# An attention and gated-MLP kernel: the scaling of p on GpSimd by two row scalars, an addition moved to GpSimd, more engines for float64 pieces, and new order tables

## The chip, the cores and the metric

The kernel runs on one core of one Trainium2 chip. The metric is the device time of one execution in microseconds. Three runs of the kernel before took 406.78, 407.47 and 408.01 us; the median is 407.47 us.

## The reference

```
# q, k, v: (4 batches, 8 heads, 768, 64) float32; n_global = 8, n_local = 96
scores = q @ k.T / 8 - slope[h] * dist     # dist: distance, n_local for global keys
scores = where(key < n_global or 0 <= row - key < n_local, scores, -1e9)
a = exp(scores - max); a = a / (sum(a) + 1e-9)
x = (a @ v) laid out as (4, 768, 512)
h = gelu_tanh(x @ w_in)                    # w_in: (512, 1024) float64
u, v = halves of h
v_n = (v - mean) / sqrt(var + 1e-6) * g_ln # layernorm over 512
v_s = w_sg @ v_n + b_sg                    # w_sg: (768, 768), over the sequence
out = x + (u * v_s) @ w_out                # w_out: (512, 512) float64
```

w_in and w_out arrive as float64 and are turned into float32 on the chip.

## The kernel before, in words

Attention is done in 48 units: a unit is one batch, one pair of heads and two blocks of 128 rows. For a unit TensorE makes the scores in 64x64 quarters (line 1115); VectorE adds the bias, finds the row's extreme and writes p (line 1147); ScalarE takes exp and the row sums (line 1152); a small operation adds 1e-9 to the sums (lines 1159 to 1163), VectorE takes the reciprocal (line 1165); and then p's four pieces, each 128 rows by 128 or 168 columns, are multiplied by it, one row scalar for each row. Each of the four may go to GpSimd (line 1174), ScalarE (line 1172) or VectorE (line 1177). In the first 16 units (`TURNS = 16`) p is then transposed by TensorE (line 1236) and copied out of PSUM (lines 1241, 1242); later units are transposed in blocks by VectorE and DMAs. The products with v are line 1264.

The gated MLP of a batch follows its attention and is mixed with the attention of the next batch. Each float32 operand is held as a high and a low part, so a product is three matmuls (lines 576 to 578). `norm` makes v's tile: gelu, statistics on VectorE (lines 633, 634), an addition of 4e-6 (line 635), the power -0.5 and a product on GpSimd (lines 640, 641), the normalization, and the split into z. The last batch's product with w_out is done by seven products of blocks instead of eight (`seven`, lines 824 to 826); its results are added up by VectorE from PSUM (line 836, and for x's low half line 717, VectorE or GpSimd) and stored (line 846).

`load_split` brings a piece of a weight matrix. A float64 piece of 256 or 512 columns is loaded as words; ScalarE multiplies the upper words by 2^-112 (line 927); the 16 bits beside are copied (line 932, GpSimd or VectorE); VectorE shifts and joins (lines 936, 938). Then any piece is cast to its high part (lines 940 to 942), and the rest becomes its low part (line 943). w_in comes in four pieces of 512 and eight of 256 columns, w_out in eight of 256.

The order of all work is planned in Python before the program is written. An operation (`op`) lists the engines that may do it, each with a busy time and a latency that the planner is told. `Plan.order` walks through time and lets each engine take the waiting operation that is due first, on the engine that would end it first. Two tables steer it, with one character for each of the 2612 operations: SHIFTS moves an operation in the order, and WAYS fixes an engine by a letter (P for GpSimd, D, A) or leaves it open with "-". Ways named DVE_SB, DVE_TS, POOL and POOL_TS count as using the port that VectorE and GpSimd share: the planner keeps such work of the two engines apart, and in the program a GpSimd operation of that kind waits for the VectorE operation before it ("beside VectorE"). POOL_FREE does not hold the port and gets no such wait. While TensorE would wait in the first 75 us, `keep_on` puts in products with a column of zeros (line 512). ALIGNED sets the address of TensorE's code at one place; HINTED places two branch hints near the end.

Of the kernel before, what the change touches and what calls it, by code (L numbers as in the profile page):

```python
# [10 lines left out]
F32 = mybir.dt.float32  # L11
# [5 lines left out]
ALU = mybir.AluOpType  # L17
PSUM = bass.MemoryType.PSUM

P = 128  # L20
# [31 lines left out]
HINTED = ("DVE", 100, mybir.EngineType.DVE), ("PE", 16, mybir.EngineType.PE)  # L52
ALIGNED = 86, 232
# [12 lines left out]
    "LJ0b0XJM0eA0ccV3WXFtrkNLJPNBzF-FhqNNAe2a0eJXbD0C201PKrBnf-6J1QojnW2wfVKTvELgvf1avq45VV30K18Hwfz2OkO5b0dc00ZN"  # L66
    "MZWw9n4-oUxuckTXWIeThmq5IKlV-50O4VtS-j0dmo94U2mZ000JHtHns-xfD4QQ67J64jZ0F57R00w4vodyM8eh09s0Do35X4F16SE1ntVO"
    "E-u4KT46E5V0ZUb8woA8RJU6RMrB0Vup-Z6rQ80doSPV5ur----8--yTKZ-t---n--v2BBt7oj00000Y4R5m5hNUzCuRldRjts7x-g-yT-nv"
    "9iQ1WZku8ml8bnSe0LswyuV0z1--l7y--C2mg--M5q--pWcx9i9V04iBLAzpTIE0Pb16sjtanFsWclFX9GLMHSZEJJKgGdI5k2-Rtjk84hMy"
    "Nr5-sPpQ-75vtIGtFFTtUrxdGbrY-KYrfadRvcS8rqlWGiWDDU3bJRJL5qz0bvcvvxxaDrt3PFRDAtRuupblR-vJQJ7uFRrmXd00M3eWtF2f"  # L70
    "1p1L23GVp18LmG4Ys1OccgKJ-h1-RBC16u8f3Y1Y-bDM-67ER5PZSI0NhhBDSRC9w3Q6aagO9l-Scgpw-Lj8YCw1crW1wl-eKRq7-sQeRx5m"
    "lFGV0ayIU5NIsUa4XNtouxHb-X0Kd3510YAcf6NB69jpSJW-smSAw0g0awTSdOVzdAZ49eaQYVaFFF68EeJYH-ubr0Bd0XWca0g-I9-F0-13"
    "16P04LPKt0w0FG160wsfiUuT-k-k7eGgZW-lcDTj8u-6qi9M3QY1F0Qlm0LoO0005038BzvdGsvT450-t--Zr--f---y-y-V-qjdUsONBnS3"
    "G9dWv-c9fU-mW0l6TlptOJX3NR-d-Oa-9NkWAOeKA6DBBgL4AABDAkFG4WpyGwaocSO-esWFHQ0O8Dccnk04rlQzmHWhYQUz-S8U0BHU07yK"
    "3krSIbGr--B7Okc-zdywZf0Z004kkA9WykrfGAfcWeWPL5Fm0OMVntcDhr069fJXhwosU2o0nxT9M9Yzrz-P-UzVfYdcvJL1CCG-1NSrOTvr"
    "d-UJshGqmYK6vJ-0Lv00f1PmjjImM1OoNNe7Bh8CJnCd0okgfs3h80Osh100nilYA9Cc7A-6bYWRMgF0SiUFBePOyz-w-qrnJFr--O-M7Xhj"
    "sUIhtF5FiG7F0T0wFt-vyWQa2Nq6skk30907DS2v09Og595u0FMa06ym8MkGj5GVKtBpvaQaXEsyTTUO80-tucRXtf9P430-7H1F-Aa90k0R"
# [8 lines left out]
    "dkknY8ndEP1Yt0MkLtb0ahHVpsxN8sy8Zbg65AG-r7Ie-I-s6PS2p-0cRUOaW5S2-cbguayZH828d1Fj---yXt--bU9X5jmAF--c0DviNbNe"
    "Uu-VGwkZO-L-EII-UeGSLd0S6pps-MdaRMbJJ-UKf02902bv-Z67vOBH0bHuzuvrZYmKpmKbnWyQs0xCxEWh5lFcHLE0X2V8K5A29308qGEu"
    "i087I-Q7j-Z7PdxtSt1alYoBiUa4ZElKzmIS0IKTW0pk9UOSO0vfKNiR7T-IcmTGxuC0jbukopGLeofaeWEWZMbsWsH00000-nG0Db0008lC"
    "kyQarbqijX5u9PFqWJuSlbBMlVl4I1BkJttKO2BQHMhJ3oNxu8YCgKIBG005JNHEcxt9GabMMLnHq20xlaakpx3T8TwFK3yDbO-lxf54UytL"
    "-G4V7OYo-eTvzcFMsY-Z"  # L90
# [27 lines left out]
    "-----D----D---------"
# [434 lines left out]
class Moe:  # L553
# [72 lines left out]
    def norm(self, t, ps):  # L626
# [85 lines left out]
    def sbuf(self, out, a, b, how, cols, reads):  # L712

        nc, op = self.nc, self.plan.op

        def one(eng):
            eng.tensor_tensor(out.ap, a(), b(), how)

        op([on_dve_sb(cols) + (partial(one, nc.vector),), on_pool(cols) + (partial(one, nc.gpsimd),)], reads, [out])
# [82 lines left out]
    def seven(self, x, dst, late):  # L802
# [13 lines left out]
        def product(n, i, left, right, on=None, after=None):  # L816
# [913 lines left out]
```

## Time and profile before

| | |
|---|---|
| median of three runs | 407.47 us |
| the profiled execution's own time | 406.97 us |
| its span, first to last instruction | 405.2 us |
| mean granted TensorE clock | 0.994 |
| TensorE busy | 396.0 us, 98% |
| VectorE busy | 345.5 us, 85% |
| ScalarE busy | 224.9 us, 56% |
| GpSimd busy | 198.9 us, 49% |

PE is TensorE's matmuls, PEld its weight loads, DVE VectorE, ACT ScalarE, POOL GpSimd and SP SyncE, which issues the DMAs. Matmuls are pipelined, and their ends are modelled, so a busy PE is not necessarily a PE at its peak. L1174 is line 1174 of the kernel.

### The profile page before, as it was taken

Reading aid. Unit: us, or ns where it says so; the run is one execution under the profiler, and the core shown is the slowest. Engines: PE = TensorE matmul, PEld = TensorE weight load, DVE = VectorE, ACT = ScalarE, POOL = GpSimd, SP = SyncE. Lnnn points to the kernel's source line nnn. Section 1 sums busy time; section 2 is a strip of 40 time slices with the busy share of each in tenths; the row PEclk is TensorE's granted clock in tenths of the full one; section 3 lists DMA queues with packets and bytes.
Section 4 is the critical chain, followed back from the end, with each engine's and each line's share of the span. In section 5 each row is a group of like instructions: output and inputs, shape, how many; then the busy total and the mean of one; then the engine's idle time right before and its main releaser. Section 6 shows DMA issues by size and latency. Waiting matters only on the chain.

```text
span 405.2 us, 12620 instructions
## 1 busy us (share of the span) xinstructions
PE 396.0 (98%) x4629; PEld 362.8 (90%) x4629; DVE 345.5 (85%) x1149; ACT 224.9 (56%) x736; POOL 198.9 (49%) x335
## 2 busy tenths in 40 slices
PE   7989999999999999999999999999999999999995
PEld 4868778999999889999999988999999888999995
DVE  7898999999998999987876989977667677878995
ACT  5899999865565657654534666725344233421300
POOL 3455788875455684332222454416221363594532
PEclk9899999999999999999999999999999999999999
DMA  7875765445878886837487665745277442000003
GB/s 231 294 177 163 232 198 169 140 130 174 258 232 264 243 274 203 247 97 232 140 255 225 199 185 153 216 111 165 64 215 245 119 141 51 20 1 2 0 21 142
DMA packets 50115, 67.14 MB, mean 166 GB/s; under 512 B 5888, under 2 KB 34048, under 8 KB 50048
## 3 DMA queue, kind: packets, MB, share of 16 engines
q1 hardware_dynamic: 50048, 66.28, 53.7%
q8 instruction: 38, 0.62, 0.7%
q14 instruction: 29, 0.24, 0.2%
HBM read 47.91 MB, written 18.35 MB: 164 GB/s over the span
## 4 chain that ended last, share of the span: by engine, by line
PE 88%; ACT 5%; DVE 4%; issue 1%; DMA 1%; POOL 0%; DVEq 0%; ACTq 0%; POOLq 0%
PE mm_ps L576 24%; PE mm_ps L578 23%; PE mm_ps L577 23%; PE av L1264 8%; PE s_ps L1115 6%; ACT p L1152 2%; PE tps L1236 2%; DVE p L1147 1%; PE mm_ps L826 1%; PE mm_ps L825 1%; PE mm_ps L824 1%; ACT p L1172 1%; DMA ni<-in_n_gl_dram 1%; ACT pt L1241 1%; ACT stage L927 1%
## 5 line engine op out<-in xcount | busy, mean ns | idle before, releaser
L1152 ACT ACTIVATE p<-p,pst 128x168 f32<-128x168 f32 (+1 forms) x192 | 80.9, 424 | 36.4 <-DVE pst L1147 35.3
L576 PE MATMUL mm_ps<-wsg,z 128*128 128x384 f32 x192 | 65.4, 340 | 0.0
L578 PE MATMUL mm_ps<-wsg,z 128*128 128x384 f32 x192 | 64.3, 335 | 0.0
L577 PE MATMUL mm_ps<-wsg,z 128*128 128x384 f32 x192 | 64.3, 335 | 0.0
L1147 DVE CUSTOM_DVE_ANT_0 p<-s_ps,bias 128x168 f32<-128x168 f32 (+1 forms) x192 | 54.3, 317 | 4.2 <-PE s_ps L1115 1.7
L1174 POOL TENSOR_SCALAR p<-p,pst 128x168 f32<-128x168 f32 (+1 forms) x87 | 40.1, 471 | 26.3 <-DVE pst L1165 20.7
L1264 PE MATMUL av<-pt,v 64*64 64x128 f32 (+1 forms) x1408 | 49.0, 253 | 0.6 <-ACT pt L1241 0.5
L1264 PEld LDWEIGHTS av<-pt,v 64*64 64x64 f32 x1408 | 37.6, 135 | 8.6 <-issue 3.7
L576 PE MATMUL mm_ps<-x,win 128*128 128x384 f32 x128 | 43.5, 340 | 0.0
L578 PE MATMUL mm_ps<-x,win 128*128 128x384 f32 x128 | 42.9, 335 | 0.0
L577 PE MATMUL mm_ps<-x,win 128*128 128x384 f32 x128 | 42.9, 335 | 0.0
L1115 PE MATMUL s_ps<-qk 64*64 64x64 f32 (+2 forms) x1408 | 38.8, 241 | 0.1
L576 PE MATMUL mm_ps<-win,x 128*128 128x512 f32 x96 | 38.8, 404 | 0.0
L578 PE MATMUL mm_ps<-win,x 128*128 128x512 f32 x96 | 37.8, 394 | 0.0
L577 PE MATMUL mm_ps<-win,x 128*128 128x512 f32 x96 | 37.7, 393 | 0.0
L576 PEld LDWEIGHTS mm_ps<-wsg,z 128*128 128x128 f32 x192 | 36.0, 188 | 1.8 <-issue 1.2
L1115 PEld LDWEIGHTS s_ps<-qk 64*64 64x64 f32 x1408 | 34.0, 135 | 3.4 <-issue 1.9
L1152 ACT ACTIVATION_READ_ACCUMULATOR p<-p,pst 128x1 f32 x192 | 36.6, 191 | 0.0
L577 PEld LDWEIGHTS mm_ps<-wsg,z 128*128 128x128 f32 x192 | 36.0, 188 | 0.3
L578 PEld LDWEIGHTS mm_ps<-wsg,z 128*128 128x128 f32 x192 | 36.0, 188 | 0.0
L593 ACT ACTIVATE u<-mm_ps 128x384 f32<-128x384 f32 x32 | 15.6, 488 | 32.7 <-PE mm_ps L578 32.4
L576 PE MATMUL mm_ps<-gt,wout 128*128 128x384 f32 x96 | 32.7, 340 | 0.0
(196 smaller groups left out, 987.7 us busy)
## 6 DMA issues: line engine op xcount, KB each, us to landing
qk<-in_qk_in_dram SPq DMA_DIRECT2D x32, 328.0 KB, 4.2
pt<-far SPq DMA_DIRECT2D x24, 384.0 KB, 4.7
v<-in_v_in_dram SPq DMA_DIRECT2D x32, 256.0 KB, 3.5
far<-tt SPq DMA_DIRECT2D x52, 96.0 KB, 2.6
qk<-in_qk_in_dram SPq DMA_DIRECT2D x16, 276.0 KB, 4.0
out_dram<-o SPq DMA_DIRECT2D x23, 192.0 KB, 3.2
far<-stage SPq DMA_DIRECT2D x44, 96.0 KB, 2.5
v<-in_v_in_dram SPq DMA_DIRECT2D x16, 192.0 KB, 3.4
```

Of the source, the lines that this page charges most:

```text
L576: mm(ps.ap, ah, bh, start=(i == 0), stop=False)
L577: mm(ps.ap, ah, bl, start=False, stop=False)
L578: mm(ps.ap, al, bh, start=False, stop=(i == n - 1))
L593: op([on_act(n) + (lambda: nc.scalar.activation(out.ap, h.ap, AF.Square, scale=math.sqrt(GELU_C * GELU_A)),)], [h], [out])
L824: mm(ah, bh, start=not on and r == 0, stop=False)
L825: mm(ah, bl, start=False, stop=False)
L1115: nc.tensor.matmul(s_ps[h][e * HQ:(e + 1) * HQ, i * W + c0:i * W + c0 + n], qk[rows, qc:qc + HQ], qk[rows, QW + k0:QW + k0 + n], start=Tru ...
L1147: nc.vector.tensor_tensor_reduce(out=p[:, g, cols], in0=s_ps[h][:, i * W:i * W + nk], in1=bias[:, 2 * j + h, w0:w0 + nk], op0=ALU.add, op1 ...
L1152: op([on_act(nk, 0.225) + (lambda p=p, g=g, cols=cols, i=i: nc.scalar.activation(p[:, g, cols], p[:, g, cols], AF.Exp, bias=st[:, 0, i, g: ...
L1174: op([on_pool_ts(nk) + (partial(scaled, lambda o, a, c: nc.gpsimd.tensor_scalar(o, a, c, 1.0, ALU.mult, ALU.mult)),), on_act(nk, 0.13) + ( ...
L1236: nc.tensor.transpose(tps[:, a * P:(a + 1) * P], pc[:, c:c + P], ident)
L1264: nc.tensor.matmul(to, v[rows, vc:vc + D], of, stop=True, skip_group_check=True, **kw)
```

## The change

- In the first 16 units the scaling of p on GpSimd multiplies by two row scalars, the reciprocal and a column of ones (`w.one`), instead of by the reciprocal and the constant 1.0; the planner is told POOL_FREE and a longer time for it. Later units keep the old form.
- The addition of 4e-6 in the layernorm moves from VectorE to GpSimd.
- The multiplication of a float64 piece by 2^-112 may also go to VectorE or GpSimd, and the copy of its 16 bits also to ScalarE.
- For the fourth product of the last batch the halves of x are added in advance into the buffer of the result (`whole_x`, not before the TensorE operation that stands just ahead of the product in the program), so that one addition from PSUM is left.
- SHIFTS, WAYS, ALIGNED and HINTED have new values. 2556 of the 2612 characters of SHIFTS differ.

```diff
-HINTED = ("DVE", 100, mybir.EngineType.DVE), ("PE", 16, mybir.EngineType.PE)
-ALIGNED = 86, 232
+HINTED = ("DVE", 101, mybir.EngineType.DVE), ("PE", 16, mybir.EngineType.PE)
+ALIGNED = 97, 139
...
-            nc.vector.tensor_scalar(rs[:, 0:1], mv[:, 1:2], 4e-6, None, ALU.add)
-
-        op([on_dve(FF, 0.40) + (stats,)], [g], [st, mv, rs])
+
+        op([on_dve(FF, 0.24) + (stats,)], [g], [st, mv])
 
         def power():
+            nc.gpsimd.tensor_scalar(rs[:, 0:1], mv[:, 1:2], 4e-6, None, ALU.add)
...
-        op([("POOL_FREE", 0.92, 1.0, power)], [mv], [rs])
+        op([("POOL_FREE", 1.14, 1.22, power)], [mv], [rs])
...
+                if r == 0 and ahead:
+                    ahead(i, [next(o for o in reversed(self.plan.ops) if o.quarters is not None)])
...
+        def whole_x(i, after):
+            kept[4, i] = self.temp("o", CH)
+            self.sbuf(kept[4, i], x_of(2 + i, 0, 0), x_of(2 + i, 0, 1), ALU.add, CH, [x[2 + i][0]], after)
+
         def fourth(i, ps):
-            o = self.temp("o", CH)
-            plus_x(o, 2 + i, 0, ps)
+            o = kept[4, i]
+            plus(o, lambda: o.ap, ps, [])
             store(o, 2 + i, 0)
...
+        def scaled(eng):
+            eng.tensor_scalar(f.ap, words()[:, :, 1].bitcast(F32), 2.0 ** -112, None, ALU.mult)
+
         op([on_act(n, 0.07) + (lambda: nc.scalar.mul(
-            f.ap, words()[:, :, 1].bitcast(F32), 2.0 ** -112),)], [raw], [f])
+            f.ap, words()[:, :, 1].bitcast(F32), 2.0 ** -112),),
+            ("DVE_TS", 0.07 + n / 1850, 0.15 + n / 1350) + (lambda: scaled(nc.vector),),
+            ("POOL_TS", 0.19 + n / 438, 0.22 + n / 438) + (lambda: scaled(nc.gpsimd),)], [raw], [f])
...
-            ("DVE_TS", 0.065 + n / 1400, 0.25 + n / 960) + (partial(beside, nc.vector.tensor_copy),)], [f], [raw])
+            ("DVE_TS", 0.065 + n / 1400, 0.25 + n / 960) + (partial(beside, nc.vector.tensor_copy),),
+            on_act(n) + (partial(beside, nc.scalar.copy),)], [f], [raw])
...
                 op([on_pool_ts(nk) + (partial(scaled, lambda o, a, c: nc.gpsimd.tensor_scalar(
-                        o, a, c, 1.0, ALU.mult, ALU.mult)),),
+                        o, a, c, 1.0, ALU.mult, ALU.mult)),) if n >= TURNS else
+                    ("POOL_FREE", 0.12 + nk / 255, 0.15 + nk / 255) + (
+                        partial(scaled, lambda o, a, c: nc.gpsimd.tensor_scalar(
+                            o, a, c, w.one, ALU.mult, ALU.mult)),),
```

The letters of WAYS that the prediction speaks of, in the order of the operations:

```
scaling of p, first 14 units (56):   before A 9, D 12, P 16, open 19    after A 21, D 14, P 6, open 15
scale of float64 pieces 0 to 7:      before ScalarE only                after DD-D--P-
copy of 16 bits, pieces 0 to 7:      before -D-DPPD-                    after -AAAA-A-
high part, w_in pieces 0 to 7:       before -AAA-AAA                    after ---A--P-
```

## Rows read from the trace of the kernel before

**Rows 1.** The page: busy us, share of the span and instructions of each engine.

```profile
PE 396.0 (98%) x4629; PEld 362.8 (90%) x4629; DVE 345.5 (85%) x1149; ACT 224.9 (56%) x736; POOL 198.9 (49%) x335
```

**Rows 2.** Busy time by stretch: start:end, length, busy time and instructions per engine.

```profile
10.00:62.00 52.00, 49.93 (x965) 40.06 (x964) 48.31 (x216) 49.63 (x180) 32.78 (x60) 0.97 0.67 209
85.00:110.00 25.00, 25.00 (x247) 24.16 (x247) 24.22 (x78) 13.61 (x45) 15.09 (x21) 1.00 0.57 173
62.00:400.60 338.60, 338.57 (x3575) 318.48 (x3573) 288.96 (x893) 169.70 (x540) 162.72 (x250) 1.00 0.52 158
```

**Rows 3.** The same view, line 512 (zero column) alone: PE and PEld.

```profile
10.00:62.00 52.00, 6.93 (x86) 5.77 (x86) 0.97 0.67 209
```

**Rows 4.** Waits: who waited for whom; us in total, times, longest.

```profile
PEld tps L1236 <- POOL p L1174: 3.0, 3, 1.8
...
PE tps L1236 <- POOL p L1174: 2.3, 2, 1.4
```

**Rows 5.** Timeline of the end: start, duration, engine, line, operation.

```profile
400.11 0.55 DVE L836 TENSOR_TENSOR kept<-kept,mm_ps 128x384 f32<-128x384 f32 x1
...
400.23 0.34 PE L826 MATMUL mm_ps<-late,wout 128*128 128x384 f32 x1
...
400.68 0.55 DVE L836 TENSOR_TENSOR o<-x,mm_ps 128x384 f32<-128x384 f32 x1
...
401.26 0.56 DVE L717 TENSOR_TENSOR o<-o,x 128x384 f32<-128x384 f32 x1
401.85 0.33 SPq L846 DMA_DIRECT2D out_dram<-o  x1
```

**Rows 6.** Scalings of p to 62 us by line: count, ns min/median/max, first and last start.

```profile
L1174 POOL TENSOR_SCALAR p<-p,pst x18: 375/410/1055, 9.3 to 57.9; 128x168 f32<-128x168 f32 x16, 128x128 f32<-128x128 f32 x2
L1172 ACT ACTIVATE p<-p,pst x20: 396/421/467, 9.2 to 58.8; 128x168 f32<-128x168 f32 x17, 128x128 f32<-128x128 f32 x3
L1177 DVE TENSOR_SCALAR p<-p,pst x18: 274/302/584, 9.5 to 55.4; 128x168 f32<-128x168 f32 x11, 128x128 f32<-128x128 f32 x7
```

**Rows 7.** Groups on POOL, 10:62: busy us, mean ns, idle before, releasers.

```profile
L1174 POOL TENSOR_SCALAR p<-p,pst 128x168 f32<-128x168 f32 x15 | 6.4, 433 | 1.9 <-DVE win L943 0.8 <-DVE pst L1165 0.7
...
L648 POOL TENSOR_SCALAR vg<-vg,mv,rs 128x512 f32<-128x512 f32 x1 | 2.1, 2091 | 0.0
...
L641 POOL TENSOR_SCALAR rs<-mv,rs 128x1 f32<-128x1 f32 x3 | 0.9, 295 | 0.3
```

**Rows 8.** Timeline, POOL and DVE side by side at 11 and at 49 us.

```profile
11.13 1.34 POOL L932 COPY stage<-stage 128x512 int16<-128x512 int16 x1 [0.29 <-ACT stage L927]
...
11.96 0.58 DVE L1177 TENSOR_SCALAR p<-p,pst 128x128 f32<-128x128 f32 x1
...
49.25 2.09 POOL L648 TENSOR_SCALAR vg<-vg,mv,rs 128x512 f32<-128x512 f32 x1
...
49.69 0.63 DVE L1177 TENSOR_SCALAR p<-p,pst 128x168 f32<-128x168 f32 x2
```

**Rows 9.** Groups on ACT, 10:62, columns as in rows 7.

```profile
L1172 ACT ACTIVATE p<-p,pst 128x168 f32<-128x168 f32 x16 | 6.5, 427 | 0.0
...
L927 ACT ACTIVATE stage<-stage 128x512 f32<-128x512 f32 x4 | 2.7, 670 | 0.0
...
L940 ACT CAST win<-stage 128x512 fp32r<-128x512 f32 x3 | 1.9, 624 | 0.0
L927 ACT ACTIVATE stage<-stage 128x256 f32<-128x256 f32 x4 | 1.6, 426 | 0.0
...
L940 ACT CAST win<-stage 128x256 fp32r<-128x256 f32 x3 | 1.2, 403 | 0.0
```

**Rows 10.** Busy time by stretch, line 932 alone: DVE, then POOL.

```profile
10.00:62.00 52.00, 2.25 (x4) 4.39 (x4) 0.97 0.67 209
```

**Rows 11.** Groups on DVE, 10:62, columns as in rows 7.

```profile
L936 DVE TENSOR_SCALAR stage<-stage 128x512 int32<-128x512 int32 x4 | 1.6, 424 | 0.2
...
L635 DVE TENSOR_SCALAR rs<-mv 128x1 f32<-128x1 f32 x3 | 0.5, 153 | 0.1
```

More of the change, by code (lines that the diff above doesn't have):

```diff
@@ L86 @@
[L86 to L90, printed above, removed]
+    "4lTyOXWL7-sM13fBP0a1V65-bt94s0KaTK95Hg0Mk--o8BiEAbV-i0G0Lgm1V6pge9Gi0pmeeRiGsrovVZbenVpC82090qhLN-rioOAutn3f"
@@ new lines @@
+    "w0JZRBp9r3b7kwjOr3U0dLn0ZBCUl-N0lcPO7UZq-zm0rXQdH2AN20gSY2qpniIsmDfXZEI8APPr-GVeTOurpoYUJvYaRc0b40BS0WB8bnf6"
+    "nwn4L109Rt0L-3Jw0XLDY4o9Lk0cJ2DSE05E340ZLHhfZFCclASWtwxdnI0nEnUQxGXnqGjQ4a8-nzNF-iqYVXzpW2p-iqYpwUSS7ww0I00H"
+    "H0FZ00DGXtGe8TC0JxSVDsydmdm-ratAieEMZA1VpW12eR-9fBGpRt2E035K2FhXXkwqTT3PKdoiG-OZ8O0HZrmHifsdqUMufauD-DBaz5L0"
+    "dg5DblMeL0XBpTK4y1a3Kma-HEebS-zv-Tu-wY4-BzCD-tFq-IIGbZyw-fgZSchlbWB8KIsZN95a0920b0hbe2kZ0bc02Ue0n0000n0LpBj1"
+    "2hTQ6FWpcr6Amh7CuiDtmYe7-8tvW4iBk-SxtkvVQMFxquUe7-flw-xOxnte6oMSZXNjmJPV6BMA7c0w-00TeYKZwclkG-t5d5FySgDJ4A4L"
@@ new lines @@
+    "XAU4Iz00abUBBJ-vZxKtAt8Bdpb0DUeQyzml-WiBG6u6zNpy-qg2Y-5NqXzfTYYZNVUm0XmQLOlgiUOJPWrDoYqRNwVE4ZWg-gTos8y-m-tX"
+    "TnlJCI0q0D48-befLOhk9SX4X407U-KWZiSW-sLPI0m0CtNEVcWHYOC0Ysal5WFhhEeIWG4Tug-DyycIVyCwz-acdF8aQvwsTDpIuT5fNibE"
+    "-toVKm1buerfSLIGZUCHuFuvaoIxjoG0SrsOxRKGyV--poYvuS7bpOFdOV0VGkSQfd70gJIR0GmBlopqn--uz-h7lmqnuoi6aYS-MjW9upDo"
+    "aWLtaksDGbC-m0AunHFv-OX6wwLdv-fz7rSTdq1-nPNEUyic1nKcXhUam6pKs6Oa-CpqOIiazzCnPgSlz41y99-AvFlb1K7a2sjWLRGdea-6"
+    "0-SfWkaSu2lCETJj6bGw7TLjN8b0W36eDDyPyyyYI6im9s5chwliVZST50vDsb9kI8dBKP5vdMMSXUvHbWGkaDvWQC7wE0jURUah-luelSXR"
@@ new lines @@
+    "tWZBVvBZgWKLKtT0ZOG93PH5U0AGGEtNWj57emqM9SeGRS0Mub02900PJKDgR0NWcPzz-Z80oQBYWFY0v-Geqz4JOVkGEr0V6ZPL--LtC-a-"
+    "cT-v8VlIn-Fqu7gJ0QUIpqidiKbXPU0wdHZ2AGKIZ-el-kAxkqNe0al3-0fLYL-RVZfaMYlHs1syVCJU05e-iAIQNMGtv1L20U3OK4Rc6xY0"
+    "2SlLDEa0doBsWfkPnD0a5NR5-0gI-71020W0E0f4ogrgTcdcamh-0N60iOjv60rVKanq202ZRRRSPFTDaW400bMeSNLSJMXUoKDgAE0dPfaC"
+    "lNeQSEmWJtAe0Ti0iidtBQufAFx-MuiBose081x0clXRY0JFeFeGAT010oRLRQ0-S3PpIbV8-HZI8-04H5O0M23K0nN0Klp03Xa0c0Doa0HK"
+    "d8cvSw8fi-9ajbhXDaQRKjJ27XhDML409RLUclQVZ0B00oB0mWGV8C045ECIG3RPhv6trx---ZlvvqpKtUSzV4ySzOeW8Zngjf-mdsR-zb6V"
@@ new lines @@
+    "OZY-Vka8OLkea-PvqXNb2UYWco0aQMXSTVkdr49MKl3VOE-3W8kg3Mns00Se-drb30-7WtR-gY-aMQPgI0gTsQ4rUEd1tBYfQJNr-0wWB3wd"
+    "aSYQMQVqX2dXToAbvgsxeJAYCZUjd7HXe33mKPl46iV0J4Hn44BpznlaZQXVpaYHp0bxHajPYI80R0N5K-bMhT7hb0Qm8dp2QxOZcPpYK4v9"
+    "SHa7--20JSBYBG4a491yrO7YXHL9SWe20T0AR080P001d5f56fV-6PzAXjYgOtphYg44efg-hglTh6RUGT0RdlZ9sld3KqGKBie0v08maeb0"
+    "lGFcVM4U0ahURdp-VJRo34ds-EkdRgut-f2G-dYZN--HP-QP-m072sfiH4AssCsNq0oPEQ3uijKHaPg5dRb76WdQj7Lfk9-ZK-UbbHInLd08"
+    "8IWOImIS-YspGSq3HsWouhyp0hfiu0YO50qT0eRCTbSjLCOHXoOGZ6p3iGXkOb66dkhE4ZZNY4--kWgFqwy655xvXH34HjHOZ-zXzlrG5Vgm"
@@ L119 @@
+    "PDPD-PP--P---D------------------------A----------------D-AP---------------D-----------------P------D---D----"
+    "-----------DDD--DPP----D---D---------------D---PPDA------------P---P-------DD-P-D-------P-PD-P--------------"
+    "--D----P------------"
 )
@@ L710, in out_tile, with sbuf @@
             lambda k: [gt[c, k], (w.wout, (k, m // 2))], 1, after)
-    def sbuf(self, out, a, b, how, cols, reads):
+    def sbuf(self, out, a, b, how, cols, reads, after=()):
         nc, op = self.nc, self.plan.op
@@ L717, in one @@
             eng.tensor_tensor(out.ap, a(), b(), how)
-        op([on_dve_sb(cols) + (partial(one, nc.vector),), on_pool(cols) + (partial(one, nc.gpsimd),)], reads, [out])
+        op([on_dve_sb(cols) + (partial(one, nc.vector),), on_pool(cols) + (partial(one, nc.gpsimd),)], reads, [out], after)
     def sums_of_w_out(self, late):
@@ L814, in of_sum, with product @@
             return lambda h, r, i: self.sums[q, r][:, h, i * P:(i + 1) * P], lambda r: self.sums[q, r]
-        def product(n, i, left, right, on=None, after=None):
+        def product(n, i, left, right, on=None, after=None, ahead=None):
             ps = banks[n, i] = banks[on, i] if on else self.bank("mm_ps", CH, SPARE)
@@ L894, in seven @@
                 7: both(7, of_sum(3), of_t(3), on=1, after=seventh),
-                4: both(4, quarter(1, 1), of_t(4), on=1, after=fourth),
+                4: both(4, quarter(1, 1), of_t(4), on=1, after=fourth, ahead=whole_x),
                 3: both(3, of_sum(4), lambda r: gt[1, 2 + r], on=5, after=third)}
@@ L960, in local_global_attention_moe @@
     nc.vector.memset(w.tiny, 1e-9)
+    w.one = small[:, 3:4]
+    nc.vector.memset(w.one, 1.0)
     nc.scalar.activation(small[:, 1:2], w.mhalf, AF.Exp)
```

71 lines of the change are left out of this document (26 added, 45 removed).

## The prediction, before the result was known

> **What bounds the kernel now.** The page first [rows 1]: TensorE counts as busy for 396.0 of 405.2 us, so a change can only win where TensorE is not busy, or is busy with nothing useful. The table of stretches says where that is [rows 2]. From 62 to 400.6 us TensorE is busy for 338.57 of 338.60 us: no work of another engine, however much cheaper, shortens this stretch by itself. From 10 to 62 us TensorE idles 52.00 - 49.93 = 2.07 us, while ScalarE is busy 49.63 of 52 us, VectorE 48.31, GpSimd 32.78. And not all of that busy time is work: the products with a constant zero column (line 512), which only keep the clock up while TensorE would wait, take 6.93 us of the same stretch [rows 3]. So about 9.0 us are lost there; ScalarE is nearest to full. The named waits of TensorE [rows 4] are small, but the two largest, 2.3 us on the matmul side and 3.0 us on the weight side, are for line 1174, the scaling of p on GpSimd. Last, the end [rows 5]: the last product starts at 400.23 and takes 0.34 us, but VectorE adds on until 401.82, and the last store is issued at 401.85; the 3.35 us to the end of the span are its landing. So three places count: the early stage (ScalarE, with GpSimd's scalings), the tail (VectorE), and in between nothing but TensorE.
>
> **The tail: -0.6 us.** Until now the fourth product of the last batch makes two additions after each bank is ready, the bank to x's high half (line 836) and then x's low half (line 717). The new code adds the halves beforehand into the same buffer (whole_x), and one addition is left. VectorE's end is a chain: 400.11 kept, 400.68 o, 401.26 o again [rows 5], each 0.55 us. With both low additions gone from the chain (that of 401.26 and its like for the bank before), VectorE catches up with TensorE: the last bank is ready at 400.23 + 0.34 = 400.57, one addition of 0.55 ends at about 401.2 instead of 401.82. That is -0.6; the lower end is 0, if the new order puts another two-step product last, and the upper -0.65, where TensorE itself is the end. The two additions of the halves are not free, but go where GpSimd has time; if VectorE gets them within the last 3 us, 0.55 each comes back.
>
> **The scalings of p: longer on GpSimd, but alone.** In the first 14 units, those finished by 62 us, GpSimd made 18 scalings, ScalarE 20, VectorE 18 [rows 6]. The new form has no row of its own; line 648 is the same operation with two row scalars, 2.091 us for 512 columns [rows 7]. In proportion, 168 columns are 0.69 us; on the line through the one-column form (line 641, 0.295 us) they are 0.88 us. I take the middle, 0.79, against 0.433 for the old form: +0.36 us each. What is bought with it: line 648 does not hold VectorE. At 49.69 two VectorE scalings run beside it in 0.63 us together, as usual (median 0.30 each [rows 6]); beside GpSimd's line 932 at 11.96 one takes 0.58 us [rows 8]. The old form is planned to wait for VectorE's port work: 1.9 us of GpSimd's idle time lies before its 15 longer scalings [rows 7]. Of the two TensorE waits of 2.3 us in all I therefore let the waiting go and the longer operation stay: -2.3 + 2 x 0.36 = -1.6. Ends: -2.3 (both gone), and +1.8, if all five waits of [rows 4] stay and each is 0.36 longer.
>
> The Trainium skill, VectorE: DVE Perf Modes, section Mode Summary, says that VectorE's second port is shared with GpSimd and that GpSimd instructions and VectorE's two-port ones block each other. The row at 11.96 agrees (0.58 against 0.30); the row at 49.69 does not for two row scalars. By the rule alone the change would hold VectorE longer, a rival below. The Trainium skill, GPSIMD Engine Reference, section Engine selection, calls one-input work roughly line-rate; by that a scaling would cost GpSimd no more than before and this sum would be -2.3. The 2.091 us of line 648 speak against it.
>
> **Who does them: ScalarE +0.6 us.** The table WAYS fixes an engine by a letter or leaves the choice to the planner. For the 56 scalings of these units the letters were 9 ScalarE, 12 VectorE, 16 GpSimd, 19 open; they become 21, 14, 6 and 15 open. Open ones in equal thirds give 26, 19, 11: ScalarE +6 x 0.427 = +2.6 us [rows 9], VectorE +0.3, GpSimd 11 x 0.79 - 18 x 0.456 (8.21 us in 18) = +0.5.
> Float64 pieces, the first eight (four of 512 columns, four of 256): ScalarE scaled all, 4 x 0.670 + 4 x 0.426 = 4.4 us. New letters: three 512s on VectorE, one 256 on GpSimd, four open (a third of them on ScalarE: 0.65). The copy between words had VectorE 2.25 and GpSimd 4.39 us [rows 10]; now ScalarE has three 512s and two 256s fixed. No such copy on ScalarE is in the trace; its casts of that width take 0.624 and 0.403 [rows 9], so 2.7, with a third of the open ones 3.2. ScalarE: -4.4 + 0.65 + 3.2 = -0.6 (ends -1.7 and +1.7). If the strided halfwords cost ScalarE what they cost VectorE (2.25 us for four [rows 10]), the result is the same.
> Casts of the weights (line 940): 3.1 us on ScalarE now; one 512 stays fixed, six are open: -1.4 (ends -2.5 and +0.6).
> ScalarE in all: 2.6 - 0.6 - 1.4 = +0.6 us; with every open one elsewhere 0.4 - 1.7 - 2.5 = -3.8, with every one on it +9.1. VectorE: scale 3 x 0.424 [rows 11] + 0.4 open, copies -2.25 + 0.6, scalings +0.3, about +0.3. GpSimd: copies -4.4 + 1.0, one scale and the additions below about +1.9, scalings +0.5: -1.0. The three engines' work hardly changes; what goes is the mutual waiting. Early stage: +0.6 - 1.6 = -1.0 us. It cannot win more than the 9.0 us lost.
>
> **The addition of the layernorm: 0.** One VectorE instruction of 0.153 us [rows 11] goes, one GpSimd instruction of about 0.3 us (line 641 is the nearest) comes, 24 times; three of them lie before 62 us. The chain to z grows by about 0.15 us; it is hidden since products of z come many us later. Without cover it would cost 0.15 once per stage. VectorE gains 3 x 0.153 = 0.46 early; after that it is not the bound, though nearly (24.22 of 25 us from 85 to 110 [rows 2]): should TensorE arrive earlier there, VectorE is late next.
>
> **Code alignment and the hint near the end** (ALIGNED, HINTED): no row prices them; TensorE has 0.03 us idle in the long stretch, so I take 0, within 0.3 either way.
>
> **Sum.** -0.6 - 1.0 = -1.6 us on the profiled execution of 406.97 (span 405.2 and 1.8 around it): 405.4. That execution lies 0.5 under the median 407.47; the forecast of the median is 405.9.
>
> **Rivals.**
> Only the tail arrives (0.21): ScalarE's share and the longer scalings eat the waits; 407.47 - 0.6 = 406.9. For it: the three engines' sum barely changes.
> Much of the early loss goes (0.13): a third of 9.0 us and the tail, 407.47 - 3.6 = 403.9. For it: GpSimd idles 19 us of these 52; against: ScalarE at 95%.
> GpSimd's longer scaling ends last in its unit (0.12): place, the wait of the transposition (line 1236) for line 1174; price 0.36 per unit, not hidden because the next products need that p. From five units on it eats the forecast's 1.6 us; with seven, +2.5 - 0.6: 409.4. For it: five waits in [rows 4]; against: only 6 fixed letters.
> ScalarE takes the open scalings as before (0.09): 11 of the 19 open went to it (20 less 9); then 30 are its, +4.2 - 0.6 - 1.4 = +2.2, less the tail: 409.1.
> The new form holds VectorE as well (0.03): 11 x 0.79 us held instead of 18 x 0.456 matters little in sum, but each of VectorE's port instructions meeting it loses up to 0.79; with four such on the path and the tail, 407.47 + 3.2 - 0.6 = 410.1. The Trainium skill's sentence on the shared port (VectorE: DVE Perf Modes, Mode Summary) would have it so.
>
> **Numbers.** The forecast has 0.42, its own range 404.9 to 406.9. A measurement tells 0.3% (1.2 us) from nothing, so faster means under 406.2: 0.8 of the forecast, the early gain, a seventh of the tail alone: 0.34 + 0.13 + 0.03 = 0.50. Slower, over 408.7: the three last rivals, 0.24. The rest, 0.26, is within. Eight in ten: 403.2 to 409.2.
>
> **What would show it.** Tail: after the last product one VectorE addition, not two, and the last store issued about 1 us after that product starts instead of 1.6. Scaling: the new line at 0.69 to 0.88 us for 168 columns, with VectorE's neighbours unstretched. Early stage: the column-of-zeros time and idle time together down from 9.0 to about 8, the end of the sparse stage at 61 instead of 62, and no wait of TensorE over 1 us for the scaling. ScalarE's busy time to 62 us tells the rival. Wrong would be: a longer early stage with ScalarE fuller, or TensorE with gaps after 62 us.

## The result and the profile after

The changed kernel takes 410.91 us (median of 5 runs, 410.48 to 411.58), the kernel before 407.47 us (5 runs, 406.09 to 408.01): 1.0094 times as long, 95% interval 1.0071 to 1.0117. The forecast was 405.9 us with a range to 409.2, so sign and range were both wrong. The profiled execution takes 410.54 us, its span 408.8 us against 405.2.

The page of the kernel after, busy us of each engine, beside [rows 1]:

```profile
PE 396.5 (97%) x4633; PEld 361.7 (88%) x4633; DVE 344.8 (84%) x1139; ACT 229.3 (56%) x740; POOL 202.3 (49%) x342
```

The sums have hardly moved, and say nothing of the cause. The stretches do (columns as in [rows 2]; the third and fourth entries after the length are VectorE and ScalarE):

```profile
10.00:62.00 52.00, 48.47 (x960) 38.74 (x959) 47.10 (x213) 50.45 (x174) 28.62 (x55) 1.00 0.64 203
62.00:85.00 23.00, 21.09 (x212) 18.38 (x210) 21.20 (x66) 22.78 (x69) 11.32 (x19) 1.00 0.51 152
85.00:110.00 25.00, 25.00 (x203) 24.02 (x194) 24.12 (x74) 18.21 (x54) 19.31 (x29) 1.00 0.62 191
```

The second of these stretches in the kernel before:

```profile
62.00:85.00 23.00, 23.00 (x221) 20.92 (x220) 22.69 (x73) 20.15 (x67) 18.48 (x31) 1.00 0.56 174
```

The same view of line 512, the products with the zero column:

```profile
10.00:62.00 52.00, 5.88 (x81) 5.31 (x81) 1.00 0.64 203
62.00:90.00 28.00, 1.65 (x8) 0.71 (x8) 1.00 0.44 131
```

To 62 us TensorE loses 3.53 us idle and 5.88 us in zero columns, 9.4 us against 9.0. The new loss is behind it, where the kernel before had next to none: 1.91 us idle from 62 to 85 us and 1.65 us of zero columns, 3.56 us. ScalarE is now full to 85 us (50.45 of 52, then 22.78 of 23). The waits of TensorE from 5 to 110 us (total, times, longest):

```profile
PEld av L1281 <- ACT pt L1258: 4.2, 7, 1.0
...
PE av L1281 <- ACT pt L1258: 2.3, 4, 0.8
...
PE mm_ps L578 <- DVE z L613: 1.4, 1, 1.4
PE tps L1253 <- DVE p L1194: 1.1, 1, 1.1
...
PE tps L1253 <- ACT p L1186: 1.0, 3, 0.7
```

The waits for GpSimd's scaling [rows 4] are gone from the matmul side; in their place TensorE waits most for ScalarE, for its copies out of PSUM (line 1258, 2.3 us) and its scalings (line 1186, 1.0 us). The longest single wait, 1.4 us at 81.5 to 82.9 us, is for z on VectorE (line 613); it is most of the idle time after 62 us, and E5 tells below whether it belongs to ScalarE too. What ScalarE does there is the copy of 16 bits, line 943 (count, ns min/median/max, first and last start):

```profile
L943 ACT COPY stage<-stage x18: 752/784/1352, 10.1 to 98.3; 128x256 int16<-128x256 int16 x14, 128x512 int16<-128x512 int16 x4
```

18 of the 20 copies are ScalarE's, at 1.33 us (mean, 512 columns) and 0.79 us (256); the forecast had 0.624 and 0.403. Ten of the 18 lie after 62 us. On ScalarE's own timeline the next instruction starts 1.06 us after the first copy:

```profile
10.07 1.31 ACT L943 COPY stage<-stage 128x512 int16<-128x512 int16 x1
11.13 0.57 ACT L1258 COPY pt<-tps 128x384 f32<-128x384 f32 x1
```

so even by what follows, not by its recorded length, a copy holds the engine for 1.06 us, and the copy out of PSUM that TensorE waits for stands behind it.

### The profile page after: what moved, and what is told of

It reads as the page before. It is cut to its first block, busy times and chain, and to the rows that moved or that the text cites. A ratio compares the mean times of both kernels' runs of the same rounds, so it can differ in the third digit from the quotient of the medians.

```text
span 408.8 us, 12621 instructions
## 1 busy us (share of the span) xinstructions
PE 396.5 (97%) x4633; PEld 361.7 (88%) x4633; DVE 344.8 (84%) x1139; ACT 229.3 (56%) x740; POOL 202.3 (49%) x342
## 4 chain that ended last, share of the span: by engine, by line
PE 56%; DVE 6%; POOL 1%; issue 0%; ACT 0%; DVEq 0%
PE mm_ps L576 16%; PE mm_ps L577 15%; PE mm_ps L578 15%; PE av L1281 4%; PE s_ps L1129 3%; PE mm_ps L825 1%; PE mm_ps L826 1%; PE mm_ps L824 1%; DVE p L1161 1%; DVE vg L598 0%; DVE st L633 0%; DVE vg L595 0%; DVE tt L1220 0%; DVE stage L1220 0%; DVE p L1194 0%; DVE y L771 0%
## 5 line engine op out<-in xcount | busy, mean ns | idle before, releaser
L1166 ACT ACTIVATE p<-p,pst 128x168 f32<-128x168 f32 (+1 forms) x192 | 80.9, 424 | 27.7 <-DVE pst L1161 22.0
L1186 ACT ACTIVATE p<-p,pst 128x168 f32<-128x168 f32 (+1 forms) x74 | 28.0, 420 | 15.0 <-DVE pst L1179 14.7
```

The source lines that it names most:

```text
L1166: op([on_act(nk, 0.225) + (lambda p=p, g=g, cols=cols, i=i: nc.scalar.activation(p[:, g, cols], p[:, g, cols], AF.Exp, bias=st[:, 0, i, g: ...
L1186: put(ps[i][:, g, cols], ps[i][:, g, cols], st[:, 2, i, g:g + 1])
```

## The experiments

Each ratio is against runs of the kernel before on the same chip (406.5 to 406.9 us there), with its 95% interval, five rounds each; a difference between two experiments on different chips is taken from their ratios.

**E1, E2: the copy elsewhere, all else in the order of the changed kernel.** E2 has `nc.vector` in place of `nc.gpsimd`.

```diff
-            on_act(n) + (partial(beside, nc.scalar.copy),)], [f], [raw])
+            on_act(n) + (partial(beside, nc.gpsimd.tensor_copy),)], [f], [raw])
```

> The changed kernel in its own planned order; only the copy of 16 bits, which the plan gives to ScalarE 18 times, is issued on GpSimd instead. Theory 1 (ScalarE's copy takes 1.33 us for 512 and 0.79 for 256 columns in the trace, where the prediction put 0.62 and 0.40, and ScalarE sets the stage to about 90 us): ScalarE loses 15.5 us of work, GpSimd gains about 16 us and has room for most of it; the time falls by 3 to 5 us to 406 to 408. Theory 2 (the new scaling form on GpSimd) and theory 3 (the new order itself, whatever the copies cost): no change, 410 to 412.

> The same copies issued on VectorE, in the same order. Theory 1: ScalarE loses 15.5 us, VectorE gains 4 x 0.755 + 14 x 0.47 = 9.6 us, and it is 91 to 96% busy there already; so a smaller gain than on GpSimd, 408 to 410. Theories 2 and 3: 410 to 412.

Measured 417.22 us (1.0263, 1.0243 to 1.0283) and 414.12 us (1.0197, 1.0175 to 1.0220): both slower still, both expectations missed. E1's groups from 5 to 90 us (count, busy us, mean ns, idle before) show why:

```profile
L1194 DVE TENSOR_SCALAR p<-p,pst 128x168 f32<-128x168 f32 x15 | 6.7, 464 | 0.1
...
L943 POOL COPY stage<-stage 128x512 int16<-128x512 int16 x4 | 5.9, 1476 | 1.6 <-DVE stage L934 1.6
...
L1194 DVE TENSOR_SCALAR p<-p,pst 128x128 f32<-128x128 f32 x6 | 3.9, 664 | 0.0
```

GpSimd's copy runs beside VectorE's scalings, which the tables no longer keep apart from it, and they take 464 and 664 ns; in E2, with the copies on VectorE, the same groups have 328 and 282 ns. Those of E1 that lie beside such a copy take 0.6 to 1.4 us each, the others 0.25 to 0.5. That agrees with the Trainium skill, Advanced Engine Details and Errata, section Mode Summary, by which GpSimd and VectorE's two-port instructions block each other; the prediction cites this rule under another page's title. In E1 TensorE waits 4.0 us for these scalings. Taking a load off ScalarE without a new order only moves the wait, so these two do not tell what the copy costs where it is.

**E3: only this in the kernel before.** All 20 copies issued by ScalarE, in the order of before.

```diff
-        op([on_pool_ts(n, 0.35) + (partial(beside, nc.gpsimd.tensor_copy),),
-            ("DVE_TS", 0.065 + n / 1400, 0.25 + n / 960) + (partial(beside, nc.vector.tensor_copy),)], [f], [raw])
+        op([on_pool_ts(n, 0.35) + (partial(beside, nc.scalar.copy),),
+            ("DVE_TS", 0.065 + n / 1400, 0.25 + n / 960) + (partial(beside, nc.scalar.copy),)], [f], [raw])
```

> The kernel before in its own planned order; all 20 copies of 16 bits are issued on ScalarE. Theory 1: ScalarE gains 4 x 1.33 + 4 x 0.79 = 8.5 us before 62 us, where it is busy for 49.6 of 52, and 9.5 us after it; VectorE and GpSimd lose 13.8. The time rises by 4 to 8 us to 411 to 416. Theories 2 and 3: within 1 us of 407.5, since neither the scaling nor the order changes.

Measured 413.74 us (1.0183, 1.0167 to 1.0200), as expected. The stretches have the changed kernel's shape, ScalarE full and TensorE idle after 62 us too:

```profile
10.00:62.00 52.00, 45.98 (x907) 36.58 (x908) 42.39 (x195) 50.71 (x174) 24.11 (x52) 1.00 0.64 204
62.00:85.00 23.00, 20.87 (x205) 17.66 (x207) 21.11 (x70) 22.03 (x66) 15.41 (x27) 1.00 0.45 139
```

**E4: the old form of scaling in the changed kernel** (six instructions).

```diff
-                            o, a, c, w.one, ALU.mult, ALU.mult)),),
+                            o, a, c, 1.0, ALU.mult, ALU.mult)),),
```

> The changed kernel in its own order; the scalings that the plan gives to GpSimd in the first 16 units (6 of them) multiply by the constant 1.0 again instead of by a second row scalar. Theory 2 (the new form is what costs): 408 to 410. Theories 1 and 3: within 0.6 us of 410.9, since 6 x (0.54 - 0.41) = 0.8 us of GpSimd's time is at stake.

Measured 411.18 us (1.0118, 1.0103 to 1.0132): no change from 410.91, so the form is not the cause.

**E5: a cheaper copy on the same engine at the same place.** Half of the columns of ScalarE's copies are left out.

```diff
-            on_act(n) + (partial(beside, nc.scalar.copy),)], [f], [raw])
+            on_act(n) + (lambda: beside(lambda a, b: nc.scalar.copy(a[:, 0:n // 2], b[:, 0:n // 2])),)], [f], [raw])
```

> The changed kernel in its own order; ScalarE's 18 copies of 16 bits copy half of the columns only (the other half is left out). Each then holds ScalarE about as long as the plan assumed: by the starts of the instructions behind them they hold it 1.07 us for 512 columns and 0.51 for 256 now, the plan has 0.48 and 0.27. ScalarE loses 4 x 0.55 + 14 x 0.25 = 5.7 us. Theory 1 (these copies on the fullest engine cost the time): most of the 3.6 us that TensorE loses from 62 to 90 us comes back, 407 to 408.5. Theory 3 (the order, whatever the copies cost): 410 to 411.

Measured 407.45 us (1.0009, 0.9996 to 1.0023). With nothing changed but the length of 18 instructions, 3.5 us come back, as expected. Its stretches:

```profile
10.00:62.00 52.00, 49.35 (x966) 39.68 (x965) 47.85 (x218) 49.44 (x181) 29.68 (x56) 1.00 0.64 208
62.00:85.00 23.00, 22.73 (x224) 20.44 (x223) 22.65 (x72) 21.58 (x69) 12.59 (x22) 1.00 0.45 143
```

TensorE's idle time from 62 to 85 us falls from 1.91 to 0.27 us, and its wait for z from 1.4 to 0.3: that wait belonged to the copies too. The length of the copies on ScalarE is therefore shown as the cause of the loss. With them halved, the rest of the change comes out at nothing, not at -1.6. The halved copies are still longer than the forecast's 0.624 and 0.403 us (ScalarE's groups from 10 to 62 us: count, busy us, mean ns, idle before), so a part of what is missing may be theirs:

```profile
L947 ACT COPY stage<-stage 128x256 int16<-128x256 int16 x4 | 3.1, 765 | 0.0
...
L947 ACT COPY stage<-stage 128x128 int16<-128x128 int16 x4 | 1.3, 534 | 0.0
```

**E6, E7: a new plan from the same tables**, without ScalarE's way (E6: the old line is left out) or with the measured price told to the planner (E7, shown).

```diff
-            on_act(n) + (partial(beside, nc.scalar.copy),)], [f], [raw])
+            ("ACT", n / 460 - 0.05, 0.24 + n / 470) + (partial(beside, nc.scalar.copy),)], [f], [raw])
```

> The changed source without ScalarE as an engine for the copy; same tables, so the order is planned anew and VectorE and GpSimd share the copies as before. Theory 1: ScalarE loses about 11 us of busy time to 100 us, 406 to 409. Theory 3 (the tables): 410 or more. A new order brings differences of its own, about 1 us.

> The changed source with one number mended: the planner is told that ScalarE's copy holds it n/460 - 0.05 us (1.06 and 0.51) and ends after 0.24 + n/470; tables as they are, so the letters still put the copies on ScalarE. If only the wrong price in the plan were the fault (the order waits for things that come late), 407 to 409; if it is the work on ScalarE itself, 410 to 412.

Measured 415.98 us (1.0228, 1.0209 to 1.0247) and 419.57 us (1.0320, 1.0307 to 1.0334). Only E6's second expectation (410 or more, from the tables) covers its time; its first and both of E7's missed. With these tables another price gives another order, and both new orders are worse. They say nothing of the copy.

**E8: the old tail in the changed kernel** (two additions after the bank again; the addition in advance shrinks to a copy of one column).

```diff
...
-            plus(o, lambda: o.ap, ps, [])
...
+                nc.vector.tensor_tensor(o.ap, xm[:, 0, :].bitcast(F32), ps.ap, ALU.add)
+                nc.vector.tensor_tensor(o.ap, o.ap, xm[:, 1, :].bitcast(F32), ALU.add)
...
```

> The changed kernel; the fourth product's result again gets x's two halves in two additions after the bank, and the addition in advance shrinks to a copy of one column. The prediction's tail term: +0.6 us, 411.3 to 411.7, the last store issued 1.2 us after TensorE's end instead of 0.7. If the tail brings nothing: 410.9.

Measured 411.28 us (1.0123, 1.0108 to 1.0139); the time alone does not separate it from 410.91. The ends do. The changed kernel's, then E8's (start, duration, engine):

```profile
404.49 0.34 PE L826 MATMUL mm_ps<-late,wout 128*128 128x384 f32 x1
404.94 0.56 DVE L838 TENSOR_TENSOR o<-o,mm_ps 128x384 f32<-128x384 f32 x1 [0.55 <-PE mm_ps L826]
405.52 0.33 SPq L848 DMA_DIRECT2D out_dram<-o  x1
```

```profile
404.00 0.34 PE L826 MATMUL mm_ps<-late,wout 128*128 128x384 f32 x1
...
404.45 0.55 DVE L884 TENSOR_TENSOR o<-x,mm_ps 128x384 f32<-128x384 f32 x1 [0.56 <-PE mm_ps L826]
405.03 0.56 DVE L885 TENSOR_TENSOR o<-o,x 128x384 f32<-128x384 f32 x1
405.65 0.33 SPq L848 DMA_DIRECT2D out_dram<-o  x1
```

From TensorE's last product to the last store it is 405.52 - 404.83 = 0.69 us with the new tail, 405.65 - 404.34 = 1.31 us with the old one, and 1.28 us in [rows 5].

**E9, E13: the tail alone in the kernel before**, its two additions made in advance on VectorE (E9) or on GpSimd (E13). The code is that of the change (`whole_x`, `ahead`) and is left out here; of the two tables, only one row each differs. E13's letters of WAYS are shown, E9 has D in place of P. Only the last products' order differs.

```diff
...
-    "-----D----D---------"
+    "--P----P------------"
...
```

> The kernel before with only the change of the tail: the halves of x added in advance for the fourth product of the last batch, all other work in the order of the kernel before up to the last products. By the prediction's step on the tail: -0.6 us (0 to -0.65), so 406.2 if the kernel before gives 406.8 in these runs; the last store is issued about 0.7 us after TensorE's last product ends instead of 1.28. The rival, that the additions made in advance take VectorE's time in the last microseconds and TensorE then waits, gives no gain, 406.8, with TensorE's end later by as much as the tail is shorter.

> The kernel before with only the change of the tail, as in e9, but with the two additions made in advance on GpSimd instead of VectorE. If e9 lost its gain to them (VectorE 0.55 us late, the last three stores close together), this gives the prediction's step back: -0.6 us, 406.2 against 406.8, with the last store issued 0.7 us after TensorE's end and 3.3 us from there to the end of the span. If the tail is worth nothing, 406.8; if e9's loss comes from the idle time near 16 us, 407.4 to 407.9 again.

Measured 407.89 us (1.0024, 1.0012 to 1.0036) and 407.36 us (1.0016, 1.0003 to 1.0029): no gain, where the forecast's step would have given 406.2. The end of E13:

```profile
399.58 0.34 PE L826 MATMUL mm_ps<-gt,wout 128*128 128x384 f32 x1
399.91 0.55 DVE L838 TENSOR_TENSOR o<-o,mm_ps 128x384 f32<-128x384 f32 x1
400.02 0.33 SPq L848 DMA_DIRECT2D out_dram<-kept  x1
400.37 0.55 DVE L838 TENSOR_TENSOR kept<-kept,mm_ps 128x384 f32<-128x384 f32 x1
400.48 0.55 SPq L848 DMA_DIRECT2D out_dram<-o  x1
401.12 0.40 SPq L848 DMA_DIRECT2D out_dram<-kept  x1
```

VectorE ends at 400.92 instead of 401.82, but three stores of 192 KB are issued within 1.1 us, and the span ends 4.28 us after the last one (405.4), where [rows 5] have 3.35. E9 has three between 401.00 and 401.93, and 4.07 us. In the changed kernel the last two are 1.1 us apart, and 3.28 us follow. So what VectorE gains here the stores' landing takes: next late was the transfer, not TensorE. That it is the closeness of the stores is read from these ends; no run moved a store alone. E9 has another loss, told below.

**E10, E11: the new form in the kernel before**, alone and with E9's tail.

```diff
...
-                op([on_pool_ts(nk) + (partial(scaled, lambda o, a, c: nc.gpsimd.tensor_scalar(
-                        o, a, c, 1.0, ALU.mult, ALU.mult)),),
+                op([on_pool_ts(nk) + (partial(scaled, lambda o, a, c, s=w.one if n < TURNS else 1.0: nc.gpsimd.tensor_scalar(
+                        o, a, c, s, ALU.mult, ALU.mult)),),
```

> The kernel before with only the form of GpSimd's scalings of p changed: in the first 16 units they multiply by two row scalars instead of one and a constant; order and engines as in the kernel before. By the prediction's step on the scalings (less waiting beside VectorE, longer by 0.36 us each): -1.6 us (-2.3 to +1.8), 405.2 against 406.8. By the rival that follows from the changed kernel (the form takes 0.57 instead of 0.43 us and still waits for VectorE in this order; its length is hidden or passed on): 406.8 to 407.6. The new instruction should take 0.54 to 0.60 us for 168 columns and VectorE's neighbours should stay at 0.30.

> The kernel before with the two parts together, the tail and the form of GpSimd's scalings. If the terms of the prediction add up: -0.6 and -1.6, 404.6 against 406.8. If only the tail counts: 406.2. If the longer form costs on TensorE's path what the tail wins: 406.8 or more.

Measured 407.76 us (1.0018, 1.0006 to 1.0030) and 408.21 us (1.0028, 1.0012 to 1.0045). E10's scalings to 62 us, beside [rows 6]:

```profile
L1176 POOL TENSOR_SCALAR p<-p,pst,small x18: 447/481/1077, 9.6 to 58.6; 128x168 f32<-128x168 f32 x16, 128x128 f32<-128x128 f32 x2
```

The median grows from 410 to 481 ns, not to 790, and TensorE's waits for them stay (2.4 us against 2.3): neither the price nor the gain of the forecast is there. E10's time also holds a gap of 1.03 us, told below, so the time alone would not tell; the waits do.

**E12: do the extra scalings on ScalarE eat the gain?** E5, and ScalarE's scalings in units 8 to 15 cut to 16 columns.

```diff
...
-                    on_act(nk, 0.13) + (partial(scaled, nc.scalar.mul),),
+                    on_act(nk, 0.13) + (partial(scaled, (lambda o, a, c: nc.scalar.mul(o[:, 0:16], a[:, 0:16], c)) if 8 <= n < TURNS else nc.scalar.mul),),
```

> The changed kernel in which ScalarE's 18 copies of 16 bits copy half of the columns, and in which ScalarE's scalings of p in units 8 to 15 scale 16 columns only (both leave out work; some 17 scalings and 3 us of ScalarE). With the half copies alone it was 407.45. If the scalings that moved to ScalarE (33 instead of 23 by 85 us) eat what the prediction wanted from the early stage, TensorE's waits there go and it comes to 405 to 406.5. If TensorE's early loss is set by something else (VectorE, the order of the tables), 407.0 to 407.8, and ScalarE's busy time falls without a gain.

Measured 406.94 us (0.9997, 0.9984 to 1.0011), between the two expectations; 0.5 us below E5, with overlapping intervals. Those of units 8 to 15 eat at most a small part; the earlier units' were not cut.

**E14 to E18: where TensorE's instructions lie.** E5, E9, E10 and E12 share a gap that no other engine explains. E5's:

```profile
16.74 0.43 PE L1281 MATMUL av<-pt,v 64*64 64x128 f32 x2 [0.81 <-issue]
```

It is 0.91 us in E9, 1.03 in E10, 0.48 in E11, 0.34 in E13, always before TensorE's 221st product (E7, in its new order, has 0.39 us before the 220th). The given kernels, which start this product at 16.6 us (before) and 16.1 us (after), have none. `addr_align` moves the place where a block of 256 instructions begins: to the zero columns of about 13.4 us in E5 and 14 us in before (place 10: E14 on E5, E16 on before) or of about 6 us (place 3: E15 on E5, E17 on before, E18 on after).

```diff
+                if o.place == 10:
+                    nc.tensor.addr_align(256, offset=0, max_nops=0)
                 if o.place == ALIGNED[0]:
```

> The changed kernel with half copies on ScalarE (as e5, 407.45; half of the copied columns are left out), with the start of TensorE's second block of 256 instructions put in front of the zero-column products of about 13.4 us, where TensorE waits for ScalarE anyway. If the idle time near 16 us is the loading of that block and starts when TensorE gets near it, the load now lies in the wait: 0.5 to 0.8 us less, 406.7 to 407.0. If the block comes at a fixed time, TensorE stands still from 13.4 to about 16 us: 408.5 to 410. If the idle time has another cause it stays at the same instruction: 407.45.

> As e14, but with the block's start put in front of the zero-column products of about 6 us; the next boundary is then 256 instructions later, at about 22 us instead of 16 us. If the idle time belongs to the boundary, none is left near 16 us and one may show near 22 us: 406.7 to 407.5. If it has another cause, it stays near 16 us: 407.45.

> The kernel before with the start of TensorE's second block put in front of the zero-column products of about 14 us. There the profile shows no idle time without a releaser, so the theory of the block's loading gives no gain, 406.8 (406.4 to 407.2); more than that if the new place makes a load visible, 407.4 to 408.

> The kernel before with the start of TensorE's second block in front of the zero-column products of about 6 us. Its profile shows no idle time at the block, so by the theory that only a visible idle time counts: 406.9 (406.4 to 407.3). If many of its executions do stand at the block (its times vary by 2 us), up to 1.0 less, as with the half copies: 405.9 to 406.4, and the kernel would be the fastest so far.

> The changed kernel with the same move. Its TensorE waits 0.46 us for ScalarE's copy of PSUM just before the block and shows no idle time at it, so by the theory that ScalarE's copies of 16 bits set the early stage: 410.9 (410.4 to 411.3). If the block's load has a part in the loss of the changed kernel: 409.9 to 410.4.

Measured: E14 410.12 us (1.0060, 1.0038 to 1.0082), E15 406.47 (0.9982, 0.9966 to 0.9997), E16 412.41 (1.0121, 1.0097 to 1.0145), E17 406.10 (0.9987, 0.9978 to 0.9996), E18 411.10 (1.0099, 1.0084 to 1.0114). E14's gap, then E16's:

```profile
16.29 0.69 PE L512 MATMUL av<-on 128*128 128x128 bf16 x8 [2.70 <-issue]
```

```profile
17.50 1.14 PE L512 MATMUL av<-on 128*128 128x128 bf16 x9 [3.53 <-issue]
```

The gap moved with the block's start, so it belongs to that start. Put into a wait it was not hidden but grew, and TensorE went on at 16.3 to 17.5 us wherever it had stopped. E14's second expectation came true in kind (its time is 0.1 above that range, and its executions scatter from 407.4 to 411.6), and E16 missed both of its own. With the start at 6 us (E15) there is no gap, and 1.1 us is won over E5, more than either expectation had.

The DMA packets in the traces show what TensorE stood for. The profile calls queue 8 an instruction queue, and by its counts it is TensorE's: in E5 38 packets of 16 KB for 9,429 recorded instructions of TensorE, weight loads and products counted singly, so 248 to a packet. The first packet within the span runs from 14.52 to 15.46 us in E5, 13.85 to 14.80 in E14 and 15.05 to 16.01 in E16, and TensorE goes on 1.28, 1.49 and 1.49 us after its end; in E7 and E9 to E13 it is 1.3 to 1.5 us too. In E15 the first packet runs from 8.00 to 9.25 us, and no gap follows. So the packet was not slow, about 1 us each time; it began late. What makes it begin is not settled: in E14 it follows a branch of TensorE at 13.12 us, taken here for a jump over the padding that `addr_align` puts in, but the gaps of E5 and E9 to E13 have no such branch before them. The Trainium skill, Runtime: NRT & Kernel Launch, section Instruction fetch mechanics, has instructions come in blocks of 256 by DMA while the block before runs, at a cost mostly hidden; the 248 to a packet agree with the 256, but here up to 3.5 us were not hidden.

E16 loses 4.9 us by its ratio, more than its gap; its mean granted clock to 62 us is 0.93 against 0.97 [rows 2]. E17, the second of its expectations, is 0.6 us under before, with an interval just clear of no change. This fits the packets: in the kernel before, too, the 221st product starts 1.55 us after the packet's end (15.08 us), although the profile puts no gap there, and in E17 it starts 1.0 us earlier, at 15.60. E18 shows that the block has no part in the loss of the changed kernel: there the 221st product starts at 16.06 instead of 16.10 us, and the time stays.

## Why the prediction was wrong, point by point

**The step that failed** is "No such copy on ScalarE is in the trace; its casts of that width take 0.624 and 0.403 [rows 9], so 2.7, with a third of the open ones 3.2" (*Who does them: ScalarE +0.6 us*). First, the size: 1.33 and 0.79 us, about twice. The three 512s and two 256s fixed there cost 3 x 1.33 + 2 x 0.79 = 5.6 us instead of 2.7, and the open ones of the first eight followed; the planner had been told 0.48 and 0.27. To 62 us ScalarE's copies take 5.3 + 2.5 = 7.8 us (four of each width) where the sum has 3.2. The nearest row was not a cast but the copy itself on other engines: GpSimd's 1.34 us for 512 columns [rows 8]. The prediction's second price, VectorE's 2.25 us for four [rows 10], was too low as well: four such copies are 2 x 1.33 + 2 x 0.79 = 4.2 us on ScalarE. Second, the sum was closed at 62 us. The first part says that from there "no work of another engine, however much cheaper, shortens this stretch"; it did not ask what dearer work does. [Rows 2] had VectorE and TensorE full from 85 us on, and ten more copies came after 62 us. E5 shows both together: 3.5 us. ScalarE's busy time to 62 us, by which the prediction wanted to tell its rivals apart, could not warn of it: it rose by 0.8 us, close to the forecast's 0.6, since an engine busy for 49.6 of 52 us has little more to give; from 62 to 85 us it rose by 2.6 (22.78 against 20.15).

**The scalings, -1.6**: wrong in both terms. In E10 the new form costs 0.07 us more, not 0.36, and the waits do not go. In the changed kernel GpSimd makes only six, at 568 ns in the mean; they went to ScalarE, 33 by 85 us where before had 23. The rule that I set aside (the Trainium skill, GPSIMD Engine Reference, section Engine selection: one-input work roughly line-rate) was nearer to the duration than the row of line 648; the gain of 2.3 that I worked out by it is not there either. One reading of the prediction was wrong, too: line 648 does hold VectorE. Two scalings of 168 columns take 0.52 us together when it does not run; the 0.63 us at 49.69 [rows 8] were not "as usual", and in the changed kernel such a pair beside line 648 (40.86 to 42.95 us) takes 0.93. The new form of 168 columns, at 37.00 us, left the one scaling beside it at 0.30. The first line is of the kernel before, the others of the changed one:

```profile
42.01 0.52 DVE L1177 TENSOR_SCALAR p<-p,pst 128x168 f32<-128x168 f32 x2
```

```profile
32.76 0.52 DVE L1194 TENSOR_SCALAR p<-p,pst 128x168 f32<-128x168 f32 x2
...
40.86 2.09 POOL L648 TENSOR_SCALAR vg<-vg,mv,rs 128x512 f32<-128x512 f32 x1
...
41.01 0.93 DVE L1194 TENSOR_SCALAR p<-p,pst 128x168 f32<-128x168 f32 x2
```

**The tail, -0.6**: right as VectorE's part of the changed kernel (0.69 against 1.31 us in E8). As a gain by itself it held in no other order: in E9 and E13 the last stores come too close together.

**The layernorm's addition, 0**: nothing speaks against it, but it was not undone alone. It takes 0.24 us each on GpSimd and lies in the chain to z. Before the z that TensorE waited for, GpSimd's part of the chain ended at 76.83 us, and ScalarE, busy with other work, took it up at 78.12, so the addition was covered there.

**Code alignment, 0 within 0.3**: too narrow for what such an address can do. E14 moves one and loses 2.1 us against E5, E16 4.9 us against before (by the ratios). The changed values of ALIGNED and HINTED themselves were not tried.

**The rivals**: "ScalarE takes the open scalings as before" (409.1) came nearest in what happened. Its condition came true, with 29 scalings on ScalarE by 62 us (it put 30), and so did its mark, a fuller ScalarE and a longer early stage; but what cost the time was the copies (E5), and cutting the scalings of units 8 to 15 brought at most 0.5 us (E12). The last rival's time, 410.1, is nearer, but its mechanism, the new form holding VectorE, is not what E4 shows: without the form the time stays. What would make the prediction wrong was named: "TensorE with gaps after 62 us".

**Open**: E5's ratio of 1.0009 stands 1.9 us above the forecast's (405.9 to 407.47). E15 gives 1.1 of it back at the block, E12 at most 0.5 at ScalarE's scalings; that the two add up was not run.

## What to carry to other kernels

Price an operation that is moved to another engine by the same operation wherever it has run, form and element type first, and by a different one of the same width last. Sum its cost over every stretch in which it occurs: a stretch in which the bounding engine never waits can lose time to a dearer neighbour, even if it can win none from a cheaper one. And a planner that holds a wrong price spends it on the fullest engine, while tables found for one plan fitted neither of the two others tried here, so a cost is measured by changing an instruction's length in the given order (E5), not by planning anew (E6, E7).

## What the runs showed of the hardware

A copy of 16-bit elements beside other words takes ScalarE 1.33 us for 512 columns and 0.79 us for 256, twice its float32 casts (0.624, 0.403). A multiplication by two row scalars takes GpSimd 0.48 us (median, 168 columns mostly) where one with a constant takes 0.41, although 512 columns took 2.09 us [rows 7]. GpSimd's subtraction and multiplication by two row scalars over 512 columns (line 648) stretched a pair of VectorE's scalings beside it from 0.52 to 0.63 and 0.93 us. At the start of a block of instructions TensorE stood still for 0.3 to 3.5 us, until 1.3 to 1.5 us after the first 16 KB packet of the instruction queue had landed (16.3 to 17.5 us of the span); with the block's start at 6 us it did not.
